# Fused attention and gated MLP: 99 long and 29 double periods in the hand-written TensorE order instead of 78 and 50

## The chip, the cores and the metric

The kernel runs on one core of one Trainium2 chip. The metric is the device time of one execution in microseconds (us). The profile names the engines PE (TensorE matmul), PEld (TensorE weight load, which overlaps PE), DVE (VectorE), ACT (ScalarE), POOL (GpSimd) and SP (SyncE, which issues most of the DMAs).

## The reference

The input x has 2048 rows of 512. Attention (32 heads of 16) and a gated MLP of width 1792 are computed from it and mixed row by row with a sigmoid gate:

```python
q, k, v = ...                                  # (x @ wqkv), 32 heads of 16
p = softmax(q @ k.T * 16 ** -0.5)              # 2048 x 2048 for each head
a = (p @ v).reshape(B, S, D) @ wo
b = (silu(x @ w1) * (x @ w3)) @ w2
g = sigmoid((x * gate_w).sum(-1, keepdims=True))
return g * a + (1 - g) * b
```

## The kernel before

**Data.** All matrices are float32. A product that must be precise is made of three float32r matmuls of high and low parts (high x high, high x low, low x high). Queries and keys carry high and low parts stacked in 48 of the rows that a head has in the array, and two guard rows keep the exponent in range, so that no row maximum is needed in the main loop.

**The main loop** interleaves two streams on TensorE. Their order is a string written by hand (lines 764 to 767), of which each letter is one step:

- Q is a score unit (`score`, line 746): for a pair of heads, 128 keys and 512 queries, two float32r matmuls (line 752), one a head, each in one half of the array's rows, write a PSUM tile S of two banks. One exponential on ACT (line 756) reads S and writes a tile p of 128 x 1024 in SBUF. S has two buffers (line 86), so a unit's weight load waits until the exponential two units earlier is through. There are 1024 units, and 8 buffers p.
- P stands for two units of the PV product (`pv`, line 736): for a unit two float32 matmuls of 17 columns (16 values and the row of ones that gives the denominator, line 740); each is two passes in the trace. Four of them, two heads by two query blocks, lie beside each other in the array's columns and add into one bank `acc`. After 16 key blocks `evac` (line 719) copies `acc` to SBUF and stores it.
- F is a work slot (`feed`, line 691). It issues one matmul in each of the two halves of the array's rows ("lanes"). The work comes in blocks from `blocks` (line 650): 24 blocks of query and key projections and 112 blocks of the MLP's gate and up products (line 413), 12 slots each, then 48 blocks of h @ w2 for 16 row tiles (line 531), 14 slots each, and 6 blocks of the output projection (line 617), 12 slots each, 2376 slots in all. A block is done first by one lane and then by the other, into one of three banks f. When the string is used up, `while feed()` (line 810) issues what is left, and then the rest of the output projection follows.

Other work hangs on the counters of this loop: loads of the next heads' queries and keys at fixed unit counts, splits of weights on POOL a fixed number of units after their load, small DVE operations and loads from lists, a few at each Q, and the loads of the pieces of h for row tile t + 2 when row tile t is through with them (`h_product`, line 527).

**The periods.** `one` is a long period: eight units, 21 work slots, and one run of the PV product for all eight (PPPP). `two` is a double period: eight units, 15 work slots, and two runs of four units each (PP, twice), with two units (QQ) between them. Between the long and the double periods stands a bridge, "QQFFF", whose two units stay two units ahead until the end. Every run of the PV product changes the array from two halves of rows to four groups of columns and back.

Of the kernel before, what the change touches and what calls it, by code (L numbers as in the profile page):

```python
# [33 lines left out]
def gated_mix_kernel(ctx: ExitStack, tc: tile.TileContext, x, wqkv, wo, w1, w3, w2, gate_w, out):  # L34
# [726 lines left out]


    NP = 8
    LONG, SHORT = 78, 50
    one = "QQFFFFFF" + "QFFF" * 5 + "QPPPP"
    two = "QFFF" * 5 + "QPPQQPP"
    order = one * LONG + "QQFFF" + two * (SHORT - 1) + "QFFF" * 4 + "QPPQPP"
    free = list(range(NP))

# [109 lines left out]
```

## Time and profile before

| | |
|---|---|
| median of 3 runs | 1406.11 us (1405.91 to 1407.34) |
| the profiled execution | 1405.92 us |
| its span, first to last instruction | 1404.1 us |
| granted TensorE clock | 1.000 |
| PE busy | 1397.0 us (99%) |
| ACT busy | 1033.6 us (74%) |
| DVE, POOL busy | 483.6 us (34%), 319.3 us (23%) |
| first score unit, last score unit start | 82.0 us, 1369.7 us |

The profiled execution's time is 1.8 us more than its span; the rest lies before and after the instructions. A row of the timeline has the start in us from the span's start, the duration, the engine, the line, the operation, what it writes and reads, and how many instructions were merged; in brackets stands the engine's idle time ahead of it and what ended it. The two matmuls of a unit, one for each half of the array, stand as x2, and so do the two of a work slot when both lanes read tiles of the same names. A matmul's recorded duration is longer than the distance to the next one, since matmuls are pipelined; distances between starts are what counts.

### The profile page before, as it was taken

The numbers are of one execution on the slowest core, as the hardware profiler recorded it, in microseconds if no ns is written. First come the engines' busy times: TensorE is split into PE (matmuls) and PEld (weight loads), VectorE is DVE, ScalarE is ACT, GpSimd is POOL, SyncE is SP. The second block draws the span as 40 slices with busy tenths as digits, with TensorE's granted clock in tenths as the row PEclk, the third lists the DMA queues.
The fourth block names the chain that finished last, engine by engine and source line by source line (L and its number), as shares of the span: only waits on it lengthen the run. The fifth ranks groups of instructions, "written<-read, shape, count | busy, mean of one in ns | idle before, by whom it ended". The sixth has DMA issues, their size and how long they took to land.

```text
span 1404.1 us, 28806 instructions
## 1 busy us (share of the span) xinstructions
PE 1397.0 (99%) x11399; PEld 821.9 (59%) x11399; DVE 483.6 (34%) x1067; ACT 1033.6 (74%) x1153; POOL 319.3 (23%) x356
## 2 busy tenths in 40 slices
PE   9999999999999999999999999999999999999998
PEld 7866556566566566565565565555545555555556
DVE  4511111564555546555454654511110110110113
ACT  4557777777777777777777777788788878877880
POOL 5113433011011101110110117331323332232240
PEclk9999999999999999999999999999999999999999
DMA  7653564343123423223333336443434443354435
GB/s 205 165 123 98 132 141 113 70 116 77 46 56 85 114 54 80 66 67 96 70 77 68 82 78 170 106 96 82 126 84 97 106 108 69 70 128 108 104 120 178
DMA packets 112670, 141.43 MB, mean 101 GB/s; under 512 B 16400, under 2 KB 70672, under 8 KB 109456
## 3 DMA queue, kind: packets, MB, share of 16 engines
q1 hardware_dynamic: 110384, 135.72, 40.1%
q10 hardware_dynamic: 2144, 3.80, 0.8%
q8 instruction: 92, 1.51, 0.5%
q14 instruction: 50, 0.41, 0.1%
HBM read 90.70 MB, written 48.76 MB: 99 GB/s over the span
## 4 chain that ended last, share of the span: by engine, by line
PE 99%; DVE 0%; ACT 0%; issue 0%; ACTq 0%
PE acc L740 33%; PE f L413 27%; PE S L752 20%; PE f L531 11%; PE S L184 2%; PE f L96 1%; PE f L98 1%; PE f L97 1%; PE f L617 1%; PE acc L338 0%; PE S L97 0%; PE S L96 0%; PE S L98 0%; PE f L158 0%; PE S L158 0%; ACT xH L161 0%
## 5 line engine op out<-in xcount | busy, mean ns | idle before, releaser
L756 ACT ACTIVATE p<-S 128x1024 f32<-128x1024 f32 x1024 | 967.8, 1027 | 300.8 <-PE S L752 300.8
L740 PE MATMUL acc<-p,V 128*17 128x512 f32 x4096 | 474.4, 594 | 0.0
L752 PE MATMUL S<-Qt,Kt 50*128 50x512 f32 x2048 | 403.7, 408 | 1.0 <-DVE V L396 0.7
L752 PEld LDWEIGHTS S<-Qt,Kt 50*128 50x128 f32 x2048 | 183.3, 184 | 185.5 <-ACT p L756 84.9
L740 PEld LDWEIGHTS acc<-p,V 128*17 128x17 f32 x4096 | 102.3, 97 | 272.5 <-issue 272.3
L444 DVE RECIPROCAL sg<-sg 128x64 f32<-128x64 f32 x448 | 209.3, 517 | 49.1 <-issue 47.0
L413 PE MATMUL f<-xH,fl 64*128 64x512 f32 x1088 | 217.5, 392 | 0.0
L413 PE MATMUL f<-xL,fh 64*128 64x512 f32 x1088 | 217.4, 390 | 0.0
L413 PE MATMUL f<-xH,fh 64*128 64x512 f32 x1088 | 217.4, 392 | 0.0
L413 PEld LDWEIGHTS f<-xH,fh 64*128 64x128 f32 x1088 | 104.4, 186 | 23.8
L413 PEld LDWEIGHTS f<-xL,fh 64*128 64x128 f32 x1088 | 104.3, 185 | 23.4
L413 PEld LDWEIGHTS f<-xH,fl 64*128 64x128 f32 x1088 | 104.6, 186 | 22.6 <-POOL fl L314 0.3
L713 DVE MEMSET tick<- 1x1 f32 x190 | 11.2, 59 | 274.5 <-PE f L531 156.1
L313 POOL CAST fh<-fr 128x512 fp32r<-128x512 f32 x34 | 21.6, 636 | 355.7 <-DMA fr<-in_B_w_dram 292.2
L436 DVE COPY gs<-f 128x512 f32<-128x512 f32 x56 | 38.7, 691 | 69.7 <-PE f L413 63.4
L531 PE MATMUL f<-xL,fh 64*128 64x512 f32 x208 | 61.8, 390 | 0.0
L531 PE MATMUL f<-xH,fl 64*128 64x512 f32 x208 | 60.8, 390 | 0.0
L531 PE MATMUL f<-xH,fh 64*128 64x512 f32 x208 | 59.8, 390 | 0.0
L531 PE MATMUL f<-xH,raw 64*128 64x512 f32 x192 | 57.3, 390 | 0.0
L442 DVE TENSOR_SCALAR sg<-sg 128x512 f32<-128x512 f32 x56 | 27.7, 494 | 82.9 <-ACT sg L441 77.6
L600 POOL TENSOR_TENSOR hx<-hx,gw 128x512 f32<-128x512 f32 x8 | 10.3, 1287 | 198.7 <-DMA gw<-r_d 188.2
L721 DVE COPY u<-acc 128x512 f32<-128x512 f32 x32 | 22.1, 692 | 94.7 <-PE acc L740 91.5
(216 smaller groups left out, 1277.0 us busy)
## 6 DMA issues: line engine op xcount, KB each, us to landing
Kt<-kH_d SPq DMA_DIRECT2D x128, 128.0 KB
h_d<-sg SPq DMA_DIRECT2D x56, 256.0 KB
sg<-h_d SPq DMA_DIRECT2D x43, 256.0 KB
fr<-in_B_w_dram SPq DMA_DIRECT2D x42, 256.0 KB
Qt<-qH_d SPq DMA_DIRECT2D x128, 64.0 KB
Kt<-kL_d SPq DMA_DIRECT2D x64, 128.0 KB
Qt<-qL_d SPq DMA_DIRECT2D x64, 64.0 KB
b_d<-y SPq DMA_DIRECT2D x16, 256.0 KB
```

Source lines behind the costliest of these rows:

```text
L96: nc.tensor.matmul(ps, sH, mH, start=first, stop=False)
L184: nc.tensor.matmul(ps[:, i, :], w[i][h][:, k, :], xs[b][:, k, :], start=n == k == 0, stop=n == 2 and k == ND - 1)
L313: nc.gpsimd.tensor_copy(hi, src)
L413: return nc.tensor.matmul(ps, w[i == 1][r, k, :], (xL if i == 2 else xH)[b][r, k, :], start=n == 0 and not second, stop=n == 3 * ND - 1 an ...
L436: nc.vector.tensor_copy(gs, ps)
L442: small.append(lambda: nc.vector.tensor_scalar(sg, sg, 1.0, None, op0=OP.add))
L444: small.append(lambda q=q: nc.vector.reciprocal(sg[:, q:q + 64], sg[:, q:q + 64]))
L531: ins = nc.tensor.matmul(ps, hs[t][q][i == 1][r, P * o:P * o + P], (w2L if i == 2 else w2H)[q][r, o, :], start=n == 0 and not second, stop ...
L721: nc.vector.tensor_copy(u, acc)
L740: nc.tensor.matmul(acc[r:r + DH + 1, :], V[:, k, 2 * j + h, :], p[:, h, :], start=k == 0, stop=k == NT - 1)
L752: nc.tensor.matmul(ps[:, h, :], Kt[i][r:r + 50, P * k:P * k + P], Qt[i][r:r + 50, t:t + 512], start=True, stop=True)
L756: nc.scalar.activation(p, ps, AF.Exp, scale=SCALE)
```

## The change

The two periods lose a work slot each, where the QQ or the last PV run has just passed: a long period has 20 (five after QQ instead of six), a double one 14 (two after the first Q instead of three). There are 99 long periods and 29 double ones, instead of 78 and 50. The number of units stays 1024, the runs of the PV product go from 78 + 2 x 50 = 178 to 99 + 2 x 29 = 157, and the string has 2387 work slots instead of 2388. The eight units of a period, its four letters P, and the end of the string are as before.

```diff
     NP = 8
-    LONG, SHORT = 78, 50
-    one = "QQFFFFFF" + "QFFF" * 5 + "QPPPP"
-    two = "QFFF" * 5 + "QPPQQPP"
+    LONG, SHORT = 99, 29
+    one = "QQFFFFF" + "QFFF" * 5 + "QPPPP"
+    two = "QFF" + "QFFF" * 4 + "QPPQQPP"
     order = one * LONG + "QQFFF" + two * (SHORT - 1) + "QFFF" * 4 + "QPPQPP"
```

The next rows are PE's program order before the change, early in the loop, from the two score units at the head of a long period on. S is the score tile, f a work bank, xH, xL and fh, fl are high and low parts of x and of a weight chunk.

```order
L752 MATMUL S<-Qt_108,Kt_111 128x512 x4
L413 MATMUL f<-xH_419,fh_644 128x512
L413 MATMUL f<-xH_241,fh_650 128x512
L413 MATMUL f<-xH_419,fl_645 128x512
L413 MATMUL f<-xH_241,fl_651 128x512
L413 MATMUL f<-xL_420,fh_644 128x512
L413 MATMUL f<-xL_242,fh_650 128x512
L413 MATMUL f<-xH_419,fh_644 128x512
L413 MATMUL f<-xH_419,fh_650 128x512
L413 MATMUL f<-xH_419,fl_645 128x512
L413 MATMUL f<-xH_419,fl_651 128x512
```

The ten rows of line 413 are five work slots; the two rows of the sixth follow before the third score unit. This is the same place with the change:

```order
L752 MATMUL S<-Qt_108,Kt_111 128x512 x4
L413 MATMUL f<-xH_419,fh_644 128x512
L413 MATMUL f<-xL_242,fh_650 128x512
L413 MATMUL f<-xH_419,fl_645 128x512
L413 MATMUL f<-xH_241,fh_650 128x512
L413 MATMUL f<-xL_420,fh_644 128x512
L413 MATMUL f<-xH_241,fl_651 128x512
L413 MATMUL f<-xH_419,fh_644 128x512
L413 MATMUL f<-xL_242,fh_650 128x512
L413 MATMUL f<-xH_419,fl_645 128x512
L413 MATMUL f<-xH_419,fh_650 128x512
L752 MATMUL S<-Qt_108,Kt_111 128x512 x2
```

The third score unit has moved up behind the fifth slot. The second place is PE's order around score units 712 to 714, which lie in a double period before the change; p is the exponentials' output:

```order
L752 MATMUL S<-Qt_108,Kt_111 128x512 x2
L740 MATMUL acc<-p_16743,V 17x512 x2
L740 MATMUL acc<-p_16748,V 17x512 x2
L740 MATMUL acc<-p_16771,V 17x512 x2
L740 MATMUL acc<-p_16787,V 17x512 x2
L752 MATMUL S<-Qt_108,Kt_111 128x512 x4
L740 MATMUL acc<-p_16798,V 17x512 x2
L740 MATMUL acc<-p_16810,V 17x512 x2
L740 MATMUL acc<-p_16836,V 17x512 x2
L740 MATMUL acc<-p_16848,V 17x512 x2
L752 MATMUL S<-Qt_108,Kt_111 128x512 x2
```

With the change the same units lie in a long period:

```order
L752 MATMUL S<-Qt_108,Kt_111 128x512 x2
L740 MATMUL acc<-p_16668,V 17x512 x2
L740 MATMUL acc<-p_16673,V 17x512 x2
L740 MATMUL acc<-p_16689,V 17x512 x2
L740 MATMUL acc<-p_16703,V 17x512 x2
L740 MATMUL acc<-p_16714,V 17x512 x2
L740 MATMUL acc<-p_16732,V 17x512 x2
L740 MATMUL acc<-p_16757,V 17x512 x2
L740 MATMUL acc<-p_16776,V 17x512 x2
L752 MATMUL S<-Qt_108,Kt_111 128x512 x4
```

Two runs of four units have become one run of eight, and the QQ between them now stands behind it. The third place is PE's order at the end of the string with the change, from the last score unit on:

```order
L752 MATMUL S<-Qt_109,Kt_112 128x512 x2
L740 MATMUL acc<-p_20899,V 17x512 x2
L740 MATMUL acc<-p_20907,V 17x512 x2
L740 MATMUL acc<-p_20915,V 17x512 x2
L740 MATMUL acc<-p_20928,V 17x512 x2
L617 MATMUL f<-wo_19967,fl_20299 128x512
L617 MATMUL f<-wo_19967,fh_20298 128x512
L617 MATMUL f<-wo_17796,fh_20298 128x512
L617 MATMUL f<-wo_17796,fl_20299 128x512
L617 MATMUL f<-wo_17796,fh_20298 128x512
L96 MATMUL f<-xH_15993,raw 128x512
```

Five matmuls of the output projection's last block (line 617) come behind the last run of the PV product. Before the change that block was through by then, and line 96 followed the run at once; four work slots in the last period find no work now.

## The prediction

> **What bounds the kernel now.** I read the page's busy times and its chain of work first, then the timeline of one period of each kind.
>
> ```profile
> span 1404.1 us, 28806 instructions
> PE 1397.0 (99%) x11399; PEld 821.9 (59%) x11399; DVE 483.6 (34%) x1067; ACT 1033.6 (74%) x1153; POOL 319.3 (23%) x356
> PE 99%; DVE 0%; ACT 0%; issue 0%; ACTq 0%
> L756 ACT ACTIVATE p<-S 128x1024 f32<-128x1024 f32 x1024 | 967.8, 1027 | 300.8 <-PE S L752 300.8
> ```
>
> TensorE is busy 99% of the span and the chain is TensorE alone. ACT is busy 74%, and all the idle time ahead of the exponentials is time in which they wait for scores. So the time is the length of TensorE's list, unless the change makes something else late. The periods' lengths come from the first score unit of each (timeline, PE alone): the second long period, the bridge, the first double period, and the last period.
>
> ```profile
> 92.55 0.50 PE L752 MATMUL S<-Qt,Kt 50*128 50x512 f32 x2
> ...
> 900.64 0.50 PE L752 MATMUL S<-Qt,Kt 50*128 50x512 f32 x2
> ...
> 909.27 0.50 PE L752 MATMUL S<-Qt,Kt 50*128 50x512 f32 x2
> ...
> 1361.17 0.50 PE L752 MATMUL S<-Qt,Kt 50*128 50x512 f32 x2
> ```
>
> 77 long periods take 900.64 - 92.55 = 808.09 us, 10.495 each. 48 double ones take 1361.17 - 909.27 = 451.90, 9.415 each. Inside a long period:
>
> ```profile
> 428.38 0.73 PE L752 MATMUL S<-Qt,Kt 50*128 50x512 f32 x4
> 428.94 0.40 PE L413 MATMUL f<-xH,fh 64*128 64x512 f32 x2
> 428.98 7.52 ACT L756 ACTIVATE p<-S 128x1024 f32<-128x1024 f32 x8 [1.92 <-PE S L752]
> ...
> 429.88 0.40 PE L413 MATMUL f<-xH,fl 64*128 64x512 f32 x2
> 430.12 0.39 PE L413 MATMUL f<-xL,fh 64*128 64x512 f32 x2
> 430.12 0.19 PEld L752 LDWEIGHTS S<-Qt,Kt 50*128 50x128 f32 x2
> 430.35 0.39 PE L752 MATMUL S<-Qt,Kt 50*128 50x512 f32 x2
> 430.57 0.39 PE L413 MATMUL f<-xH,fh 64*128 64x512 f32 x2
> ...
> 434.98 0.39 PE L752 MATMUL S<-Qt,Kt 50*128 50x512 f32 x2
> ...
> 438.86 0.50 PE L752 MATMUL S<-Qt,Kt 50*128 50x512 f32 x2
> ```
>
> A slot is 0.232 us (430.35 to 434.98 are 20 slots, 4.63), behind QQ 0.236 (428.94 to 430.12 are five). The two kinds of period differ by six slots, 1.39, and one run of the PV product: 10.495 - 1.39 - 9.415 = -0.31, so a run more costs 0.31 beside its matmuls. That is what 21 fewer runs would save, some 6.5 us. But ACT is near its limit where TensorE issues Q and three F: 0.927 us a unit there, and the eight exponentials above follow each other at (7.52 - 1.03) / 7 = 0.927, one period's pace set by PE. What ACT can do alone stands in the bridge, which has only three slots behind QQ:
>
> ```profile
> 900.64 0.73 PE L752 MATMUL S<-Qt,Kt 50*128 50x512 f32 x4
> ...
> 901.25 7.45 ACT L756 ACTIVATE p<-S 128x1024 f32<-128x1024 f32 x8 [2.44 <-PE S L752]
> ...
> 902.32 0.18 PEld L752 LDWEIGHTS S<-Qt,Kt 50*128 50x128 f32 x2 [0.68 <-ACT p L756]
> ...
> 902.66 0.40 PE L531 MATMUL f<-xL,raw 64*128 64x512 f32 x1
> ...
> 903.14 0.40 PE L531 MATMUL f<-xH,fl 64*128 64x512 f32 x1
> ...
> 903.24 0.19 PEld L752 LDWEIGHTS S<-Qt,Kt 50*128 50x128 f32 x2
> 903.38 0.39 PE L752 MATMUL S<-Qt,Kt 50*128 50x512 f32 x2
> ...
> 907.09 0.40 PE L752 MATMUL S<-Qt,Kt 50*128 50x512 f32 x2
> ```
>
> Here exponentials stand back to back at (7.45 - 1.03) / 7 = 0.917, and the third unit's weight load waits for ACT: it starts at 902.32, **1.68 after QQ**. The first exponential starts 0.61 after QQ and takes 1.03, so the load follows its end by 0.04. This is the edge that the change runs into.
>
> **The change part by part.**
>
> *Periods exchanged.* 21 double periods become long ones: 21 x (10.495 - 9.415) = **+22.7 us**. This holds before any period gets shorter. Long periods are then 99, double ones 27 beside the bridge and the last period.
>
> *A slot less behind QQ, 99 times.* Left to itself it gives 0.236. The third unit's load now starts with the sixth slot, 430.12, 1.74 after QQ. It would start with the fifth, 429.88, 1.50 after QQ; the exponential that holds its S buffer allows 1.68. So the load is 0.18 late. What a late load costs shows where a work slot waited for POOL:
>
> ```profile
> 822.49 0.39 PE L413 MATMUL f<-xH,fh 64*128 64x512 f32 x2
> 822.70 0.19 PEld L413 LDWEIGHTS f<-xH,fl 64*128 64x128 f32 x2 [0.25 <-POOL fl L314]
> 822.72 0.48 PE L413 MATMUL f<-xH,fl 64*128 64x512 f32 x2
> 823.04 0.39 PE L413 MATMUL f<-xL,fh 64*128 64x512 f32 x2
> ```
>
> The load came 0.21 after the slot before it began, and the next slot but one began 0.34 after the load. Undisturbed it stands two slots, 0.46, behind; here 0.55, a loss of 0.09. In the bridge the distance from load to next slot is 0.34 too (902.32 to 902.66). So about 0.12 of lateness is free and the rest is paid: 0.18 - 0.12 = 0.06 here. From the first slot behind the third unit to the last unit the bridge takes 907.09 - 902.66 = 4.43, the long period 434.98 - 430.57 = 4.41. There the loads are late as well but inside the free part (903.24 is 0.10 behind its slot), and ACT gains 0.01 a unit on PE. That is 0 to 0.02 more. A long period so gains 0.236 - 0.06 less up to 0.02, that is 0.16 to 0.18; without the rounding of the rows it could be 0.187. I take 0.175: 99 x 0.175 = **-17.3 us** (bounds -15.8 and -18.5).
>
> *A slot less behind the first Q, 27 times.* The double period:
>
> ```profile
> 1109.52 0.50 PE L752 MATMUL S<-Qt,Kt 50*128 50x512 f32 x2
> ...
> 1110.12 5.66 ACT L756 ACTIVATE p<-S 128x1024 f32<-128x1024 f32 x6 [0.54 <-PE S L752]
> ...
> 1111.26 0.19 PEld L752 LDWEIGHTS S<-Qt,Kt 50*128 50x128 f32 x2
> 1111.48 0.39 PE L752 MATMUL S<-Qt,Kt 50*128 50x512 f32 x2
> ```
>
> The unit that needs the S buffer of 1109.52 loads its weights at 1111.26. One slot sooner is 1111.03; the exponential from 1110.12 ends at 1111.15, and 0.04 more is 1111.19. That is 0.16 to 0.17 late, a loss of 0.05. The pace is as above. Of 0.232 some 0.165 stays (0.15 to 0.18): 27 x 0.165 = **-4.5 us** (-4.1 to -4.9).
>
> *The end.* Five single-lane matmuls of the last block come behind the last run, 5 x 0.23 = 1.15. Four slots ahead of it stand empty, but with fewer slots between units PE only waits for ACT there, so I credit 0.1 of a possible 0.9: **+1.0 us** (0.3 to 1.2). The list then continues with matmuls that need no result of the loop's end.
>
> *At nothing.* The bridge is at ACT's pace already. The MLP's h products start at unit 651 instead of 624 and then meet long periods, whose slots pass faster: 42 slots of a row tile take 2.1 periods, some 21.7 us, not 2.8 x 9.415 = 26.4. The pieces of h that they read are covered by the double buffer: the third row tile's last piece was split at
>
> ```profile
> 939.28 0.73 POOL L495 TENSOR_TENSOR fl<-sg,fh 128x256 fp32r<-128x256 f32 x1
> ...
> 950.78 0.40 PE L531 MATMUL f<-xL,raw 64*128 64x512 f32 x2
> ```
>
> 11 us ahead of that row tile's start at 950.78, against 4.7 us less in all. With that cover gone, each row tile in a long stretch would wait for what is missing; I put 0 to 0.5 us there. The run of a long period needs no exponential late: the eighth above ends at 428.98 + 7.52 = 436.50, and its unit is read in the last quarter of the run between 434.98 and 438.86, from some 437.9 on.
>
> Sum: 22.7 - 17.3 - 4.5 + 1.0 = **+1.9 us**. On the profiled execution's 1405.92 that is 1407.8; the median of the runs shown is 0.19 higher, so 1408.0. The change is break-even at a gain of (22.7 + 1.0) / 126 = 0.188 us a period, just over what I find.
>
> **The rivals.**
>
> *Nothing is late, faster.* If S were free in time, each period would gain its whole slot: 99 x 0.236 + 27 x 0.232 = 29.6, and 22.7 - 29.6 + 1.0 = -5.9, on the median 1400.2. For it speaks that the long loop nowhere waits for ACT now. Against it stands the row of 902.32: the same load with the same two units ahead of it cannot start before 1.68. Chance 0.08.
>
> *A late load is paid in full, slower.* The place is the same load; the price is the whole 0.18 of lateness. The gain is then 0.06 a period: 22.7 - 126 x 0.06 + 1.0 = +16.1, 1422.2. It decides if a load cannot be hidden below the 0.23 that it has now. Against it stand 822.70, where 0.21 cost 0.09, and 903.24, only 0.14 ahead of its matmul with no gap. Chance 0.05.
>
> *The exponentials are slower when they are dense, slower.* The group of line 756 has 967.8 / 1024 = 0.945 a unit. At that pace the last unit's load waits for the sixth exponential: 0.60 + 5 x 0.945 + 1.03 + 0.04 = 6.40 after QQ, its matmul 0.11 behind at 6.51, against 6.60 now (434.98 - 428.38). The gain is 0.09: 22.7 - 126 x 0.09 + 1.0 = +12.4, 1418.5. Against it: 0.917 in the bridge; 0.945 holds the single ones and the ones without a follower too. Chance 0.05. The Trainium skill's page "ScalarE: Activation LUTs", section "What ACT_TABLE_LOAD costs", has 186 ns + 0.833 ns an element for an ACTIVATE with immediate operands and about 93 ns of overlap, an estimate of 0.946 us for 1024; by it this rival would hold. The bridge's 0.917 does not agree, and the measurement decides.
>
> **How the numbers follow.** The forecast has 0.82. Its own ends are 22.7 - 18.5 - 4.9 + 0.3 = -0.4 and 22.7 - 15.8 - 4.1 + 1.2 + 0.5 = +4.5, on the median 1405.7 to 1410.6. The rows are rounded to 0.01, which is up to 126 x 0.01 = 1.3 on each side: 1404.4 to 1411.9. The rivals, 0.18, stay outside. A measurement can tell about 0.2%, 2.8 us. Faster by more is the first rival and a little: 0.10. Slower by more is the other two, 0.10, and the forecast's upper part, where a long period gains under 0.166, about a quarter: 0.32 in all. Within 0.2%: 0.58.
>
> **What would show it.** Long periods of 10.32 us and double ones of 9.25, equal over the whole loop; 157 waits of the exponentials behind PV runs instead of 178; third units' weight loads at 1.68 after QQ; exponentials at 0.917 behind QQ. Wrong would be long periods of 10.26 (first rival), or of 10.4 (the other two), or a stretch of unequal periods from unit 651 on (pieces of h late).

## The result and the profile after

The changed kernel takes 1410.28 us (median of 8 runs, 1409.91 to 1411.27), the kernel before on the same chip 1406.28 us (8 runs, 1405.91 to 1407.34): a ratio of 1.0029, 95% interval 1.0018 to 1.0040. It is slower by 4.0 us, where +1.9 was forecast.

The profiled execution took 1409.91 us. First the page's span, busy times, share of the chain by engine and the exponentials' group, all of the kernel after:

```profile
span 1408.0 us, 28786 instructions
PE 1400.8 (99%) x11399; PEld 798.5 (57%) x11399; DVE 486.0 (35%) x1067; ACT 1020.9 (73%) x1153; POOL 318.2 (23%) x356
PE 99%; ACT 0%; DVE 0%; issue 0%; ACTq 0%
L756 ACT ACTIVATE p<-S 128x1024 f32<-128x1024 f32 x1024 | 955.8, 1050 | 315.9 <-PE S L752 315.5
```

On this page almost nothing seems to have happened: TensorE 99% busy, the chain TensorE alone. ACT is even less busy, 1020.9 against 1033.6 us, although it does the same 1024 exponentials. Their mean went from 1027 to 1050 ns while their summed busy time fell: they overlap more, being back to back more often. The waits say the same (waiter <- releaser: us in total, times, longest), of the kernel after:

```profile
ACT p L756 <- PE S L752: 315.5, 157, 9.1
PEld S L752 <- ACT p L756: 86.0, 234, 0.9
```

and of the kernel before, the second of these rows:

```profile
PEld S L752 <- ACT p L756: 84.9, 100, 0.9
```

The exponentials wait 157 times, once for each PV run, as forecast. The weight loads of scores now wait for ACT 234 times instead of 100, though the total hardly moves. In the double periods two loads, each behind a run of the PV product, wait some 0.85 us whatever the change does; with fewer double periods there are 56 of these waits instead of 98, and in their place each of the 99 long periods has one of some 0.23 us ahead of its third unit. A load that waits need not hold up a matmul, so what this costs must be read from the distances between matmuls. The first score unit of the second long period, the bridge, the first double period and the last two periods (timeline after, PE):

```profile
92.56 0.50 PE L752 MATMUL S<-Qt,Kt 50*128 50x512 f32 x2
...
1105.50 0.50 PE L752 MATMUL S<-Qt,Kt 50*128 50x512 f32 x2
...
1114.08 0.50 PE L752 MATMUL S<-Qt,Kt 50*128 50x512 f32 x2
...
1354.64 0.51 PE L752 MATMUL S<-Qt,Kt 50*128 50x512 f32 x2
...
1363.92 0.50 PE L752 MATMUL S<-Qt,Kt 50*128 50x512 f32 x2
```

98 long periods take 1105.50 - 92.56 = 1012.94 us, **10.336** each (10.495 before, 10.32 forecast). 27 double ones take 249.84, 9.253 each (9.415 before, 9.25 forecast). The bridge takes 8.58 (8.63 before). From the last period's first unit to the end it is 1408.05 - 1363.92 = 44.1 us, before 1404.09 - 1361.17 = 42.9.

So the difference of the spans is made up of: 21 periods exchanged, 21 x 1.080 = +22.7; 98 long periods shorter by 0.1585 (the first long one starts together with other work and shows no gain), -15.5; 27 double ones by 0.161, -4.4; the end +1.2; bridge and start together under 0.05. The sum is **+4.0**, and the spans (1408.05 and 1404.09) differ by 3.96. A long period after, the 61st:

```profile
702.20 0.73 PE L752 MATMUL S<-Qt,Kt 50*128 50x512 f32 x4
...
702.83 2.86 ACT L756 ACTIVATE p<-S 128x1024 f32<-128x1024 f32 x3 [1.89 <-PE S L752]
...
703.70 0.39 PE L413 MATMUL f<-xH,fl 64*128 64x512 f32 x2
703.90 0.19 PEld L752 LDWEIGHTS S<-Qt,Kt 50*128 50x128 f32 x2 [0.25 <-ACT p L756]
703.93 0.47 PE L752 MATMUL S<-Qt,Kt 50*128 50x512 f32 x2
...
704.24 0.39 PE L413 MATMUL f<-xL,fh 64*128 64x512 f32 x2
...
704.82 0.19 PEld L752 LDWEIGHTS S<-Qt,Kt 50*128 50x128 f32 x2 [0.16 <-ACT p L756]
...
708.65 0.41 PE L752 MATMUL S<-Qt,Kt 50*128 50x512 f32 x2
```

The third unit's load starts 1.70 us after QQ and names ACT as what it waited for; without a wait it would start with the slot of 703.70. Its own matmul is in time, but the slot behind it starts at 704.24 and not at 704.16. The fourth unit's load waits for ACT too. The three exponentials follow each other at (2.86 - 1.03) / 2 = 0.915. The last unit comes at 6.45, where 6.60 less a slot would be 6.36.

### The profile page after: what moved, and what is told of

It is laid out like the page before. It is cut to its first block, busy times and chain, and to the rows that moved or that the text cites. A ratio compares the mean times of both kernels' runs of the same rounds, so it can differ in the third digit from the quotient of the medians.

```text
span 1408.0 us, 28786 instructions
## 1 busy us (share of the span) xinstructions
PE 1400.8 (99%) x11399; PEld 798.5 (57%) x11399; DVE 486.0 (35%) x1067; ACT 1020.9 (73%) x1153; POOL 318.2 (23%) x356
## 4 chain that ended last, share of the span: by engine, by line
PE 99%; ACT 0%; DVE 0%; issue 0%; ACTq 0%
PE acc L740 33%; PE f L413 27%; PE S L752 20%; PE f L531 11%; PE S L184 1%; PE f L96 1%; PE f L617 1%; PE f L98 1%; PE f L97 1%; PE acc L338 0%; PE S L98 0%; PE S L96 0%; PE S L97 0%; PE f L158 0%; PE S L158 0%; ACT p L756 0%
## 5 line engine op out<-in xcount | busy, mean ns | idle before, releaser
L756 ACT ACTIVATE p<-S 128x1024 f32<-128x1024 f32 x1024 | 955.8, 1050 | 315.9 <-PE S L752 315.5
L752 PE MATMUL S<-Qt,Kt 50*128 50x512 f32 x2048 | 410.5, 416 | 1.2 <-DVE V L396 0.7
L413 PE MATMUL f<-xH,fl 64*128 64x512 f32 x1088 | 223.0, 392 | 0.0
L413 PE MATMUL f<-xH,fh 64*128 64x512 f32 x1088 | 223.0, 392 | 0.0
L413 PE MATMUL f<-xL,fh 64*128 64x512 f32 x1088 | 222.4, 391 | 0.0
L413 PEld LDWEIGHTS f<-xH,fh 64*128 64x128 f32 x1088 | 108.1, 186 | 17.4
L413 PEld LDWEIGHTS f<-xH,fl 64*128 64x128 f32 x1088 | 108.1, 186 | 17.2
L550 DVE SCALAR_TENSOR_TENSOR y<-f,omg,y 128x512 f32<-128x512 f32 x32 | 24.0, 751 | 117.6 <-PE f L531 117.6
L531 PE MATMUL f<-xH,fl 64*128 64x512 f32 x208 | 61.4, 391 | 0.0
L531 PE MATMUL f<-xL,fh 64*128 64x512 f32 x208 | 61.3, 391 | 0.0
L531 PE MATMUL f<-xH,fh 64*128 64x512 f32 x208 | 59.4, 391 | 0.0
L531 PE MATMUL f<-xH,raw 64*128 64x512 f32 x192 | 53.4, 391 | 0.0
```

What stands on the lines that cost most here:

```text
L413: return nc.tensor.matmul(ps, w[i == 1][r, k, :], (xL if i == 2 else xH)[b][r, k, :], start=n == 0 and not second, stop=n == 3 * ND - 1 an ...
L531: ins = nc.tensor.matmul(ps, hs[t][q][i == 1][r, P * o:P * o + P], (w2L if i == 2 else w2H)[q][r, o, :], start=n == 0 and not second, stop ...
L550: nc.vector.scalar_tensor_tensor(y, ps, omg[:, t:t + 1], y, op0=OP.mult, op1=OP.add)
L752: nc.tensor.matmul(ps[:, h, :], Kt[i][r:r + 50, P * k:P * k + P], Qt[i][r:r + 50, t:t + 512], start=True, stop=True)
L756: nc.scalar.activation(p, ps, AF.Exp, scale=SCALE)
```

## The experiments

**Theory:** in a long period, ACT's exponentials (0.917 each, back to back) make the score units' weight loads late; about 0.12 us of a lateness is hidden and the rest is lost on TensorE. **Rivals:** a late load is paid in full; the loss lies in something else than the exponentials (pieces of h, the denser work slots); the loss belongs to one place behind QQ and another place for the removed slot avoids it.

### Shorter exponentials

The exponentials leave out 1/8 of their columns (the last 128 of 1024 keep a constant that is set ahead of the loop), first in the changed kernel, then in the kernel before, and 1/16 in the changed one. So part of the softmax is left out of the result; everything else stands.

```diff
-        p = wk.tile([P, 2, 512], F32, name=f"p{n}")
-        nc.scalar.activation(p, ps, AF.Exp, scale=SCALE)
+        p = held[n]
+        nc.scalar.activation(p.rearrange("p h t -> p (h t)")[:, 0:896], ps.rearrange("p h t -> p (h t)")[:, 0:896], AF.Exp, scale=SCALE)
...
+    held = [wk.tile([P, 2, 512], F32, name=f"p{n}") for n in range(NP)]
+    for p in held:
+        nc.gpsimd.memset(p[:, 1, 896-512:512], 1.0)
```

> The changed kernel with each exponential on 896 of its 1024 columns; the other 128 columns of p hold ones from before the loop, so an eighth of the exponentials is left out of the result. An exponential of 512 columns takes 0.62 us and one of 1024 takes 1.03, so 128 columns less should take some 0.10 us away. Theory (the third unit's weight load waits for the exponential that holds its S buffer): the load may start some 1.58 us after QQ instead of 1.68, 0.08 behind its slot, inside the free 0.12. Long periods then fall from 10.336 to 10.26-10.28 us, double ones from 9.252 to 9.18-9.20, and the time from 1410.3 to 1400.5-1403 us. Rival (the order of matmuls itself costs TensorE the time, ACT is not waited for): periods and time as in the changed kernel, 1410 us.

> Control: the kernel before with the same shorter exponentials (an eighth left out). Theory: TensorE alone sets its pace, so long periods stay at 10.49 us, double ones at 9.41, and the time within 0.1% of 1406.3 us. Rival (ACT holds TensorE back in the kernel before too): periods shorter by more than 0.02 us, time under 1403 us.

> The changed kernel with exponentials on 960 columns (a sixteenth left out). Some 0.05 us less: the third unit's load may start 1.63 us after QQ, 0.13 behind its slot. Theory (some 0.12 us of lateness is free, the rest is paid): long periods 10.27-10.30 us, time 1401-1405 us, most of the gain of 896 columns. Rival (all of the lateness is paid): half of the gain of 896 columns, long periods near 10.31 us, time near 1406-1407 us.

Measured: the changed kernel with 896 columns 1401.13 us (ratio to the kernel before 0.9965, interval 0.9951 to 0.9978), long periods 10.258 in the mean, double ones 9.19. The kernel before with 896 columns 1406.06 (1.000, 0.9991 to 1.0009), long periods 10.494. The changed one with 960 columns 1402.52 (0.9974, 0.9964 to 0.9984), long periods 10.274. Of the run with 896 columns, timeline, first the first score units of the second long period and of the bridge, 98 long periods apart, and then part of a long period:

```profile
92.25 0.50 PE L752 MATMUL S<-Qt,Kt 50*128 50x512 f32 x2
...
1097.49 0.50 PE L752 MATMUL S<-Qt,Kt 50*128 50x512 f32 x2
```

```profile
256.32 0.73 PE L752 MATMUL S<-Qt,Kt 50*128 50x512 f32 x4
...
257.82 0.40 PE L413 MATMUL f<-xL,fh 64*128 64x512 f32 x2
257.89 0.19 PEld L752 LDWEIGHTS S<-Qt,Kt 50*128 50x128 f32 x2
258.06 0.40 PE L752 MATMUL S<-Qt,Kt 50*128 50x512 f32 x2
258.30 0.40 PE L413 MATMUL f<-xH,fh 64*128 64x512 f32 x2
```

Here the load is only 0.07 behind its slot, and matmuls follow each other without a gap (257.82, 258.06, 258.30): a lateness of 0.07 costs nothing. With 960 columns:

```profile
256.90 0.73 PE L752 MATMUL S<-Qt,Kt 50*128 50x512 f32 x4
...
258.41 0.40 PE L413 MATMUL f<-xL,fh 64*128 64x512 f32 x2
258.53 0.19 PEld L752 LDWEIGHTS S<-Qt,Kt 50*128 50x128 f32 x2 [0.16 <-ACT p L756]
258.64 0.40 PE L752 MATMUL S<-Qt,Kt 50*128 50x512 f32 x2
258.88 0.39 PE L413 MATMUL f<-xH,fh 64*128 64x512 f32 x2
```

The load is 0.12 behind its slot and waits for ACT by the row's own words, and still the next two matmuls are in time. So a removed slot is worth 10.495 - 10.258 = 0.237 if the exponentials are out of the way, and the exponentials take 10.336 - 10.258 = **0.078** of it, 99 x 0.078 = 7.7 us. The kernel before does not gain from shorter exponentials: TensorE alone set its pace. That the loss lies in other work, such as the pieces of h or the denser slots, is ruled out: this work is the same with the shorter exponentials, and the loss is gone.

### One slot fewer still

```diff
-    LONG, SHORT = 99, 29
-    one = "QQFFFFF" + "QFFF" * 5 + "QPPPP"
-    two = "QFF" + "QFFF" * 4 + "QPPQQPP"
+    LONG, SHORT = 120, 8
+    one = "QQFFFF" + "QFFF" * 5 + "QPPPP"
+    two = "QF" + "QFFF" * 4 + "QPPQQPP"
```

> One step further the same way: 120 long periods with 19 slots (four behind QQ) and 8 double ones with 13. Theory: the third unit's load still cannot start before 1.68 us after QQ, so the removed slot gives nothing; long periods stay at 10.31-10.34 us, double ones at 9.23-9.26; 21 x 1.084 = 22.8 us more than the changed kernel: 1431-1434 us. Rival (TensorE's own list sets the period): each period another 0.23 us shorter, 1402-1404 us.

Measured: 1441.53 us, ratio 1.0252 (1.0236 to 1.0268). The median of the long periods is 10.33, the same as with one slot more, and so are the places of the last unit's load (6.27 us after QQ in both, medians) and matmul (6.44 and 6.45): the second removed slot is worth nothing, as expected. The changed kernel's long period already stands on what ACT allows. But the total is 7.5 us over the upper end of what was expected. Two periods are much longer, the ones from 217.5 us (14.49) and from 966.4 us (12.78). The first, timeline of that run:

```profile
219.74 0.35 SPq L175 DMA_DIRECT2D qL_d<-gs  x1
...
223.25 0.39 PE L413 MATMUL f<-xL,fh 64*128 64x512 f32 x2
...
225.34 0.69 DVE L424 COPY gs<-f 128x512 f32<-128x512 f32 x1 [4.63 <-DMA qL_d<-gs]
225.98 0.06 DVE L713 MEMSET tick<- 1x1 f32 x1
226.09 0.80 PE L413 MATMUL f<-xH,fh 64*128 64x512 f32 x2 [2.45 <-DVE tick L713]
```

Read it from below: the matmul waits for a `tick`, the memset with which `feed` hands a block from one lane to the other. The tick does no work, but it stands in DVE's queue behind a copy, and the copy waits 4.63 us for a store out of its buffer gs. The profile also has the granted clock at 0.50 from 225.9 to 229.3 us, right behind this wait: 3.4 us at half the clock are an estimated 1.7 us lost, and 10.33 + 2.45 + 1.7 = 14.48 is about the period's 14.49. The second stall is of the same kind, with another instruction ahead of the tick:

```profile
973.47 0.55 DVE L577 RECIPROCAL dd<-dd 128x64 f32<-128x64 f32 x1 [2.76 <-DMA dd<-d_d]
...
974.51 0.06 DVE L713 MEMSET tick<- 1x1 f32 x1
...
974.71 0.47 PE L531 MATMUL f<-xL,raw 64*128 64x512 f32 x1 [2.07 <-DVE tick L713]
```

Behind this one the granted clock stayed at 1.00. The two and some shorter ones are about 7 us. The changed kernel itself has no such stall: its long periods are 10.30 to 10.37, but for the first (10.57) and two of 10.43 and 10.44.

### The lateness by itself

The kernel before, nothing removed; one or two slots of a long period move from behind QQ to later places.

```diff
-    one = "QQFFFFFF" + "QFFF" * 5 + "QPPPP"
+    one = "QQFFFFF" + "QFFF" * 4 + "QFFFF" + "QPPPP"       # one slot moved
+    one = "QQFFFF" + "QFFF" * 3 + "QFFFF" * 2 + "QPPPP"    # two slots moved
```

> The kernel before with its 78 long and 50 double periods and every slot kept; in the long ones one slot is moved from behind QQ to ahead of the last unit (five slots behind QQ, four behind the seventh unit). Nothing is removed, so the time over before is the price of the lateness alone, 78 times. The third unit's load is late by 0.18 us. Theory (0.12 is free, the rest is lost, and up to 0.02 on later loads): 0.06 to 0.08 a period, +4.7 to +6.2, 1411 to 1412.5 us, long periods 10.555 to 10.575. Rival one (a late load is paid in full): +14, 1420. Rival two (a lateness of 0.18 is free, and the changed kernel's loss comes from its density over the whole period, which is not raised here): 1406.3, long periods 10.495.

> The same with two slots moved: four behind QQ, and four behind the sixth and the seventh unit. The third unit's load is late by 0.41 us. Theory: 0.41 - 0.12 = 0.29 lost, 0 to 0.03 more on later loads: +22.6 to +25, 1429 to 1431.5 us, long periods 10.785 to 10.815. Rival one (paid in full): +32, 1438. Rival two (only the density over the whole period counts): no loss, 1406.3.

Measured: one slot 1417.41 us (1.0083, 1.0069 to 1.0097), two slots 1434.42 (1.0200, 1.0187 to 1.0214). The medians of the long periods are 10.57 and 10.81 us, 0.07 and 0.32 more than the 10.495 of before, both as the theory had them; paid in full would be 0.18 and 0.41, and a loss that hangs on density alone none. With two slots moved, timeline:

```profile
734.04 0.74 PE L752 MATMUL S<-Qt,Kt 50*128 50x512 f32 x4
...
735.31 0.40 PE L413 MATMUL f<-xH,fh 64*128 64x512 f32 x2
735.75 0.19 PEld L752 LDWEIGHTS S<-Qt,Kt 50*128 50x128 f32 x2 [0.48 <-ACT p L756]
735.75 0.50 PE L752 MATMUL S<-Qt,Kt 50*128 50x512 f32 x2
736.09 0.39 PE L413 MATMUL f<-xH,fl 64*128 64x512 f32 x2
```

The load stands 1.71 after QQ, as it did with one slot less, since the exponential has not moved; the slot before it has. From load to next slot it is 0.34 again. The totals, 1417.41 and 1434.42, are over the expected 1411 to 1412.5 and 1429 to 1431.5, in the profiled executions mostly for another reason: in both, the sixth long period has a stall like those above, 2.9 and 2.5 us. With one slot moved:

```profile
141.95 0.69 DVE L424 COPY gs<-f 128x512 f32<-128x512 f32 x1 [4.94 <-DMA qL_d<-gs]
142.58 0.06 DVE L713 MEMSET tick<- 1x1 f32 x1
...
142.69 0.50 PE L413 MATMUL f<-xH,fh 64*128 64x512 f32 x2 [2.68 <-DVE tick L713]
```

With one slot moved, that accounts for the profiled execution (1414.75, its span 8.8 over that of before: 78 x 0.077 by the mean of the undisturbed long periods is 6.0, and 2.9). The other four executions of that kernel took 1417.1 to 1418.6, at a mean granted clock of 0.997 to 0.998 where the profiled one had 1.000. If the missing share is time at half the clock, as behind the stall at 226 us above, it makes an estimated 2.8 to 4.2 us, about the 2.4 to 3.8 that they are longer. This is not shown, since only one execution was profiled: some profiles have the clock at 0.50 in the last 1 to 2 us too, and with two slots moved the two executions at 0.998 are only 0.4 to 1.6 us longer than the three at 1.000.

### The slot taken elsewhere

99 and 29 periods as in the change, the removed slot taken behind the third unit, or two units ahead of the last; the latter leaves twelve single-lane matmuls at the end instead of five.

```diff
-    one = "QQFFFFF" + "QFFF" * 5 + "QPPPP"
-    two = "QFF" + "QFFF" * 4 + "QPPQQPP"
+    one = "QQFFFFFF" + "QFF" + "QFFF" * 4 + "QPPPP"            # behind the third unit
+    two = "QFFF" + "QFF" + "QFFF" * 3 + "QPPQQPP"
+    one = "QQFFFFFF" + "QFFF" * 3 + "QFF" + "QFFF" + "QPPPP"   # two units ahead of the last
+    two = "QFFF" * 3 + "QFF" + "QFFF" + "QPPQQPP"
```

> The changed kernel's 99 long and 29 double periods with as many slots, but the removed slot is taken one unit later: six slots again behind QQ, two instead of three behind the third unit; likewise three and then two in a double period. The third unit's load is then in time, as before (1.74 us after QQ against 1.68 allowed), and the fourth unit's is late instead: its own time is 2.43 us after QQ, the second exponential ends at 0.61 + 1.03 + 0.917 = 2.56, and 0.05 more is 2.61. Theory (a load is late wherever the slot is taken, because eight exponentials need 0.917 each; 0.12 of a lateness is free, the rest is lost, and what comes behind adds less here, with one unit fewer to come): long periods 10.31 to 10.33, 1407.5 to 1410 us. Rival (the loss is special to the load behind QQ, where the exponential starts late): long periods 10.26, 1401 to 1403. Second rival (two late loads add up): 10.36 or more, 1412 or more.

> The same with the removed slot taken two units ahead of the period's last one, in both kinds of period. Twelve single-lane matmuls are left behind the last run instead of five, 1.6 us. Theory: the load is late by about 0.17 there (ACT gains 0.01 a unit on PE up to that place), 0.05 is lost, and fewer units come behind: long periods 10.30 to 10.32, in all 1408 to 1410.5 us. Rival one (special to the load behind QQ): long periods 10.26, 1403 to 1405. Rival two (the loss is the same wherever the slot goes, set by the last unit's load alone): 10.336, 1411.5 to 1412.5.

Measured: behind the third unit 1410.77 us (1.0032, 1.0020 to 1.0045), long periods 10.340 (median); ahead of the last 1412.10 (1.0041, 1.0027 to 1.0055), long periods 10.324. The first missed the theory's 10.31 to 10.33 and its 1407.5 to 1410 us, and is no better than the changed kernel. The second is a little over the theory's 10.30 to 10.32 and missed its 1408 to 1410.5 us; it lies in the 1411.5 to 1412.5 of the rival by which the loss is the same wherever the slot goes, though its 10.324 is not that rival's 10.336. (Six of its long periods take 10.43 to 10.62, 1.4 us in all, and their cause was not followed up.) With the slot taken behind the third unit, timeline:

```profile
702.71 0.74 PE L752 MATMUL S<-Qt,Kt 50*128 50x512 f32 x4
...
705.15 0.40 PE L413 MATMUL f<-xH,fl 64*128 64x512 f32 x2
705.33 0.19 PEld L752 LDWEIGHTS S<-Qt,Kt 50*128 50x128 f32 x2 [0.22 <-ACT p L756]
705.39 0.44 PE L752 MATMUL S<-Qt,Kt 50*128 50x512 f32 x2
705.67 0.39 PE L413 MATMUL f<-xL,fh 64*128 64x512 f32 x2
```

The third unit is in time now (1.975 us after QQ, median), the fourth unit's load is late, and again the slot behind it comes 0.34 after the load. So the rival that the place behind QQ is special (long periods of 10.26) falls too. What fell of the theory is that fewer units behind the late load would make it clearly cheaper: by the medians the loss is 0.065 to 0.08 at all three places. Wherever the slot is taken, the last unit's load starts 0.05 us after the end of the sixth exponential (medians: 6.27 after 6.21 with the slot taken behind QQ, 6.30 after 6.25 behind the third unit, 6.34 after 6.29 ahead of the last). That this load sets the loss is not shown: it stands only 0.05, 0.08 and 0.13 us behind the slot ahead of it.

### Each part alone

```diff
+    LONG, SHORT = 85, 43      # only the double periods shortened; one is as before
+    one = "QQFFFFFF" + "QFFF" * 5 + "QPPPP"
+    two = "QFF" + "QFFF" * 4 + "QPPQQPP"
+    LONG, SHORT = 94, 34      # only the long ones shortened; two is as before
+    one = "QQFFFFF" + "QFFF" * 5 + "QPPPP"
+    two = "QFFF" * 5 + "QPPQQPP"
```

> One part alone: only the double periods are shortened, 85 long periods with 21 slots as before and 43 double ones with 14. Theory: 7 exchanged periods at 1.080 are +7.6, 41 shortened ones at 0.163 are -6.7, and five matmuls behind the last run +1.2: +2.1, 1408.4 us (1407.5 to 1409.5); long periods 10.495 as before, double ones 9.25. Rival (in the changed kernel the double periods' gain is partly paid by the long ones, or the other way round): double periods other than 9.25 by 0.03 or more, and the time other by over 1.2 us.

> The other part alone: only the long periods are shortened, 94 with 20 slots and 34 double ones with 15 as before, which leaves nothing behind the last run. Theory: 16 exchanged periods at 1.080 are +17.3, 94 shortened ones at 0.159 are -14.9: +2.3, 1408.6 us (1407.5 to 1409.8); long periods 10.336, double ones 9.415. Rival: as in the run with the double ones alone.

Measured: 1408.75 and 1408.71 us, both with a ratio of 1.0017 (1.0008 to 1.0026) to the kernel before's 1406.40: +2.35 and +2.3, where +2.1 and +2.3 were expected. Long periods 10.500 and double ones 9.250 (medians) in the first, 10.340 and 9.413 in the second; one long period of the first takes 11.17, and why was not followed up. The parts don't disturb each other, and neither is a gain by itself: no version of these beats the kernel before.

## Why the prediction came out as it did

The direction and the mechanism held; the loss is twice the forecast one, mostly by one term. The time lies inside the stated range, but not in its likeliest part: a ratio within 0.2% had a chance of 0.58, slower by more one of 0.32, and 0.29% was measured.

- *Periods exchanged, +22.7.* Held; both parts alone, with 7 and 16 exchanges at that price, came out within 0.3 us.
- *A slot less behind QQ, -17.3.* **The mis-sized term: -15.5 measured**, 1.8 us of the 2.1 that are missing. The step that failed is the choice in "That is 0 to 0.02 more. A long period so gains 0.236 - 0.06 less up to 0.02, that is 0.16 to 0.18", of which "I take 0.175" puts what comes behind the first late load at next to nothing. The first late load was sized right, 0.06. Behind it 0.01 is added by the medians, and by the means the whole loss is 0.078. (The first long period, which shows no gain, is 0.2 us of the difference.) The medians over the long periods show where (matmul of a unit, us after QQ; the run with 896 columns stands for a period without lateness):

| unit | no lateness | after | lost |
|---|---|---|---|
| third | 1.740 | 1.737 | 0 |
| fourth | 2.663 | 2.726 | 0.063 |
| sixth | 4.527 | 4.581 | 0.054 |
| eighth | 6.382 | 6.446 | 0.064 |
| next QQ | 10.259 | 10.333 | 0.074 |

  The loss of the first late load is not won back, and 0.01 more comes between the last unit and the next QQ. The forecast had the bound of 0.16 for the gain and took a value near the other end of the range. The measured 0.1585 is even a little under it.
- *A late load costs what exceeds 0.12.* Held, and now over a range. How late the first late load of a period starts (against the start of the slot ahead of it, where it starts when nothing is late), and what the next unit lost, from the medians:

| kernel | late | lost | free |
|---|---|---|---|
| after, 896 columns | 0.07 | 0 | |
| after, 960 columns | 0.12 | 0.01 | 0.11 |
| slot behind the third unit | 0.15 | 0.04 | 0.11 |
| after | 0.18 | 0.06 | 0.12 |
| slot ahead of the last | 0.18 | 0.05 | 0.13 |
| two slots moved | 0.41 | 0.29 | 0.12 |

- *A slot less behind the first Q, -4.5.* -4.4 measured.
- *The end, +1.0.* +1.2 measured. The five single-lane matmuls behind the last run, timeline after:

```profile
1372.66 2.29 PE L740 MATMUL acc<-p,V 128*17 128x512 f32 x16
1374.88 0.49 PE L617 MATMUL f<-wo,fl 64*128 64x512 f32 x1
1375.22 0.62 PE L617 MATMUL f<-wo,fh 64*128 64x512 f32 x2
1375.68 0.39 PE L617 MATMUL f<-wo,fl 64*128 64x512 f32 x1
1375.91 0.39 PE L617 MATMUL f<-wo,fh 64*128 64x512 f32 x1
1376.24 0.50 PE L96 MATMUL f<-xH,raw 128*128 128x512 f32 x1
```

  They take 1376.24 - 1374.88 = 1.36 up to the next product, where 1.15 were reckoned; the credit of 0.1 for the four empty slots is not told apart from that.
- *At nothing.* Held nearly: the bridge is 8.58, and the long periods from unit 651 on are 10.344 in the mean against 10.335 ahead of it, 0.2 us in all, where 0 to 0.5 were allowed. (The h products before the change start at about unit 620, not 624; nothing hangs on it.)
- *The rivals.* "Nothing is late" would have had long periods of 10.26: they come with the shortened exponentials alone, and with them 1401.1 us, near its 1400.2. "Paid in full" and the exponentials at 0.945 would have had 10.4; the exponentials behind QQ end 0.917 apart, long period after long period. From the figures of the Trainium skill's page "ScalarE: Activation LUTs", section "What ACT_TABLE_LOAD costs", an estimate of 0.946 us follows for them; the 0.915 of the row at 702.83 does not agree with it. The break-even of 0.188 us a period held as well: 0.159 and 0.161 are under it, and the kernel is slower.

## What to carry to other kernels

When two engines' paces are within a few per cent (here 0.927 against 0.917 us a unit), a slot taken from the slower one's list need not be won whole: work out where the other engine's pace lets the next units start, and expect the gain to stop there. Here it stopped at 10.32 to 10.34 us a period wherever the slot was taken, and a second slot gave nothing. What a first late load loses was not won back here before the next period, and a little more was added; so take the end of the range that counts the later loads. A hand-over that goes through an in-order queue of another engine works only until a shifted order puts a waiting instruction ahead of it: look at what stands in that queue before changing the order.

## What the runs showed that was not expected

- In these runs a weight load that waited for another engine came 0.11 to 0.13 us late without cost, although the profile names the wait; what was beyond that was lost (0.18 late: 0.06 lost, 0.41 late: 0.29 lost).
- From the start of the first load of a period that is 0.12 us late or more to the second matmul behind it (the slot after the unit) it is 0.34 us in the changed kernel and with slots moved alike, and so it is in the bridge of the kernel before.
- The busy time of ACT fell by 12.7 us with the same instructions, and the mean of an exponential rose by 23 ns, without ACT being faster or slower: back to back, the records overlap.
- A one-element memset on DVE stopped TensorE for 2.1 to 2.7 us, when it stood behind an instruction that waited for a transfer: once each in the runs with one and two slots moved, twice in the one with two slots fewer. Behind one of these stops, of 2.45 us, the granted clock was 0.50 for 3.4 us; behind the others that were profiled, of 2.07 to 2.68 us, it stayed at 1.00.
